# Five of the second pair's eight sets of block sums, made on GpSimd beside the qkv products

## The chip, the cores and the metric

The kernel runs on one core of one Trainium2 chip. The metric is device time in microseconds (us) of one execution. The core's engines are TensorE (PE in the profile: matrix products, with the weight loads listed apart as PEld), VectorE (DVE), ScalarE (ACT), GpSimd (POOL) and SyncE (SP). An engine works through its own instructions strictly in the order in which they stand in its program. A transfer (DMA) is issued by an engine as one of its instructions and then moves on its own; SP does hardly anything but issue transfers.

## The reference

All arrays are fp32: S = 2048 rows, D = 512 columns, Fh = 896.

```python
x  = A_x
xn = layernorm(x)
# s: attention, 32 heads of 16, each row looks at itself and 7 rows before it, 2 apart
q, k, v = split(xn @ wqkv)
logits = einsum("bhsd,bhswd->bhsw", q, k[window]) * scale     # masked before row 0
o  = einsum("bhsw,bhswd->bhsd", softmax(logits), v[window])
s  = o @ wo
# g: gated MLP
z  = gelu_tanh(xn @ w_in)
z1 = z[..., :Fh]
z2 = layernorm(z[..., Fh:])
g  = einsum("ts,bsf->btf", w_sp, z2) + b_sp                    # 2048 x 2048 times 2048 x 896
g  = silu((z1 * g) @ w_out)
out = x + s * g
```

## The kernel before

**Precision.** PE multiplies in a rounded fp32 format. Each operand is therefore split in two (`split`, line 190): ACT copies the high part (line 191), DVE subtracts it to get the low part (line 192), and a product is three matmuls (high by high, high by low, low by high).

**Stages, as PE sees them.** First an opening with the statistics of the rows and the transposes of x, and the products for q, k and v (`qkv`), whose results go to HBM as `qkv_d`. Then the first projection (z1, lines 661 to 682), which stores z1. Then the second projection (z2, lines 692 to 764), whose results are normalised and added up to the combinations that the spatial product needs. Then the spatial product (`g`, `block_product`, matmuls on line 786), then the product with w_out (`b`, line 1009 to 1020), and last `o @ wo` with the final sum (`s`, lines 1046 to 1070).

**The spatial product.** It is done in a scheme of seven block products instead of eight, m1 to m7, for two pairs a = 0, 1 of column blocks of w_sp, in the order m1a m1b m2a m2b m6a m6b m7a m7b m4a m4b m5a m5b m3a m3b. Some of the block products take plain blocks of w_sp (tiles `wsp_...`), the others take sums of blocks (tiles `ws_...`). The sums are made beforehand and kept in HBM as `sums_d`. One set of sums (pair a, index i of eight) loads four blocks of 128x512, makes four DVE additions of 128x512 and stores four results.

**Where the sums are made.** `block_sums(0, i)` for the first pair stands in the loop of the first projection: one set after each f, and the last after the first f; the tiles `sa_...`, `sb_...` are from a wide pool of eight tiles. `block_sums(1, i, False)` for the second pair stands in the loop of the second projection (line 751), one set for each i. Its tiles, `sr_...`, come from the pool `raws`, which has only four buffers ("raw"). `fetch` (line 166) takes one of these buffers and issues the load on SP (line 168). The same four buffers serve the plain blocks and sums of the spatial product (`wsp_...r`, `ws_...r`), the blocks of w_out and wo, and the attention's results on their way to the last stage (`ol`). A set of raw sums takes all four, until its stores have read them.

**The attention.** It runs on DVE, with the first fold of each step on POOL, from q, k, v that are read back from `qkv_d`. There are 32 steps. The large instructions of a step, 128x2048 each, are the product of keys and queries (`pr`, line 523), its reduction (`lg`, line 530) and the product of weights and values (`pv`, line 567); smaller ones are on lines 545 to 561 and 577 to 590. A step's result goes to HBM as `o_d` (issued by SP, line 593). The attention's work has low priority: a scheduler that sorts the program when it is built puts it where it finds DVE free, and the order is fixed then. Its results are needed only by `load_o` (line 766), the operands of the last stage. The last stage takes the row groups in the order 1, 3, 0, 2, and group 3 needs the very last steps of the attention.

**Memory.** The tiles of the opening come from a pool `tmp`: row tiles of x (`t2`, tag "t2", four buffers of 128x512) and others. This memory is released on line 473, and the wide pool and the attention's pool are laid in it. A tile in released memory waits for what used the memory before.

Of the kernel before, what the change touches and what calls it, by code (L numbers as in the profile page):

```python
# [14 lines left out]
ALU = mybir.AluOpType  # L15
AX = mybir.AxisListType

P = 128
S, D, F = 2048, 512, 1792
# [3 lines left out]
NT = S // P  # L23
KB = D // P
FB = FH // P
NG = 3
CT = 512
# [30 lines left out]
def kernel(  # L58
# [16 lines left out]
    def pin(ins):  # L75
        return tc.keep_in_program_order(ins) if pins[0] else ins
# [67 lines left out]
        return t.rearrange("p (k q) -> p k q", k=n)  # L144

    def t2(name, dt=F32, tag="t2", bufs=4):
        return tmp.tile([P, D], dt, tag=tag, name=name, bufs=bufs)

    def t35(name, dt=F32, wide=False):
        return tmp.tile([P, 2 * GC], dt, tag="t35", name=name, bufs=3)[:, : 2 * GC if wide else FH]  # L150
# [42 lines left out]
        return first_  # L193

    def load_x(j):
        xt = t2(f"x_{j}")
        pin(nc.sync.dma_start(xt, xr[j]))
        return xt

# [59 lines left out]
    def rows_ready(j0, j1):  # L259
        v = mvx[:, j0:j1, 1]  # L260
        pin(nc.vector.tensor_scalar(v, v, EPS, None, op0=ALU.add))
        pin(nc.gpsimd.tensor_tensor(v, v, nhalf.to_broadcast([P, j1 - j0]), op=ALU.pow))

    def rows_in(j0, j1):
        mr = ep.tile([P, 4, 2, P], F32, tag="mr", name=f"mr_{j0}", bufs=2)[:, : j1 - j0]
# [23 lines left out]
    def opening(wg):  # L289
        def high(k):  # L290
            hi, lo = weight_pair(f"wqkv_0_{k}")
            pin(nc.scalar.activation(hi, raw[k], AF.Copy))
            wg[k] = hi, lo

        def low(k, eng):
            pin(eng.tensor_tensor(wg[k][1], raw[k], wg[k][0].bitcast(F32), op=ALU.subtract))

        left = [12, 12]

        def times(j, *kab):  # L300
            for k, a, b in kab:
                pin(nc.tensor.matmul(
                    first[j], xn_at(j)[a][:, k], wg[k][b],
                    start=left[j] == 12, stop=left[j] == 1,
                ))
                left[j] -= 1

        x = [load_x(0)]
        raw = [fetch(wqkv[:, 0, 0, :], GC, "wqkv_0_0")]
        x.append(load_x(1))  # L310
        raw += [fetch(wqkv[:, 0, k, :], GC, f"wqkv_0_{k}") for k in (1, 2)]
        raw.append(t35("wqkv_0_3r")[:, :GC])
        pin(nc.sync.dma_start(raw[3], wqkv[:, 0, 3, :]))
        x.append(load_x(2))
        stats_x(0, x[0])
        high(0)
        normal_x(0, x[0])
        low(0, nc.vector)
        p = turned_x(0, x[0])
        stats_x(1, x[1])  # L320
        low_x(0, p)
        high(1)
        normal_x(1, x[1])
        rstd_x(0)
        low(1, nc.vector)
        high(2)
        low(2, nc.gpsimd)
        keep_warm(2)
        first.append(mm("qkv_0_0"))
        times(0, (0, 0, 0), (0, 0, 1))  # L330
        p = turned_x(1, x[1])
        high(3)
        stats_x(2, x[2])
        low(3, nc.gpsimd)
        times(0, (0, 1, 0), (1, 0, 0), (1, 1, 0), (1, 0, 1), (2, 0, 0), (2, 1, 0))
        low_x(1, p)
        normal_x(2, x[2])
        rstd_x(1)
        first.append(mm("qkv_0_1"))
        times(1, *[(k, 0, 0) for k in range(KB - 1)], (0, 0, 1), (1, 0, 1))  # L340
        times(0, (3, 0, 0), (3, 1, 0), (2, 0, 1))
        p = turned_x(2, x[2])
        times(1, (3, 0, 0), *[(k, 1, 0) for k in range(KB)], (2, 0, 1))
        times(0, (3, 0, 1))
        times(1, (3, 0, 1))
        x += [load_x(j) for j in range(3, OPEN)]
        for j in range(OPEN, OPEN + 4):
            fetch_rows(j)
        raw1 = [fetch(wqkv[:, 1, k, :], GC, f"wqkv_1_{k}") for k in range(3)]
        raw1.append(t2("wqkv_1_3r", tag="tz", bufs=2))  # L350
        pin(nc.sync.dma_start(raw1[3], wqkv[:, 1, 3, :]))
        for j in range(3, OPEN):
            xt = x[j]
            stats_x(j, xt)
            low_x(j - 1, p)
            normal_x(j, xt)
            if j - 1 < JC:
                rstd_x(j - 1)
            first.append(mm(f"qkv_0_{j - 1}"))
            left.append(12)  # L360
            times(j - 1, *[(k, 0, i) for i in range(2) for k in range(KB)])
            p = turned_x(j, xt)
            times(j - 1, *[(k, 1, 0) for k in range(KB)])
            row_stats(OPEN + j - 3)
        low_x(OPEN - 1, p)
        for j in range(10, 13):
            fetch_rows(j)
        for j in range(6, 10):
            fetch_cols(j)
        rows_ready(6, 9)  # L370
        rows_out(6, 9)
        return raw1

    def product(g, j, wg):
        xh, xl = xn_at(j)
        pq = mm(f"qkv_{g}_{j}")
        for k in range(KB):
            wh, wl = wg[k]
            nc.tensor.matmul(pq, xh[:, k], wh, start=k == 0, stop=False)  # L379
            nc.tensor.matmul(pq, xh[:, k], wl, start=False, stop=False)  # L380
            nc.tensor.matmul(pq, xl[:, k], wh, start=False, stop=k == KB - 1)  # L381
        return pq

    zpad = tmp.tile([PAD, CS], F32, tag="zpad", name="zpad", bufs=1)
    nc.vector.memset(zpad, 0.0)
# [40 lines left out]
    pair(1, 0)  # L426
    for j in range(13, NT):
        row_stats(j)
    rows_ready(13, NT)
    column_tile(8)  # L430
    low_x(7, cols[7])
    fetch_cols(12)
# [5 lines left out]
    column_tile(10)  # L438
    low_x(9, cols[9])
    pair(1, 4)  # L440
    for j in range(11, NT):
        if j + 2 < NT:
            fetch_cols(j + 2)
        column_tile(j)
        low_x(j - 1, cols[j - 1])
        if j % 2:
            pair(0, j - 5)
# [184 lines left out]

    attention()

    def pair_tiles(a, i):
        top, low = t4(f"sa_{a}_{i}"), t4(f"sb_{a}_{i}")
        nc.sync.dma_start(top, w_sp[2 * a : 2 * a + 2, i].rearrange("c p t -> p c t"))
        nc.sync.dma_start(low, w_sp[2 * a : 2 * a + 2, HT + i].rearrange("c p t -> p c t"))
        return top, low, [top[:, 0], top[:, 1], low[:, 0], low[:, 1]]

    def raw_tiles(a, i):
        return [
            fetch(w_sp[2 * a + c, r + i], CT, f"sr_{a}_{i}_{c}_{r}") for r in (0, HT) for c in range(2)
        ]

    def block_sums(a, i, whole_pairs=True):
        if whole_pairs:
            top, low, ts = pair_tiles(a, i)
        else:
            ts = raw_tiles(a, i)  # L650
        t0, t1, l0, l1 = ts
        for out_, p_, q_ in ((l1, t1, l1), (t1, t0, t1), (t0, t0, l1), (l0, t0, l0)):
            nc.vector.tensor_tensor(out_, p_, q_, op=ALU.add)
        if whole_pairs:
            nc.scalar.dma_start(sums_d[a, 0, i], top)
            nc.scalar.dma_start(sums_d[a, 1, i], low)
        else:
            for n, t in enumerate(ts):
                nc.scalar.dma_start(sums_d[a, n // 2, i, :, n % 2], t)

    for f in range(FB):
        wh, wl = prep(w_in1[:, f, :], KB * P, f"w1_{f}")
        for c in range(NC):
            pz = mm(f"z1_{f}_{c}")
            for k in range(KB):
                cc = slice(k * P, (k + 1) * P)
                xh, xl = [planes[:, FB - KB + k, c * JC : (c + 1) * JC, a] for a in range(2)]
                nc.tensor.matmul(pz, wh[:, cc], xh, start=k == 0, stop=False)  # L668
                nc.tensor.matmul(pz, wh[:, cc], xl, start=False, stop=False)  # L669
                nc.tensor.matmul(pz, wl[:, cc], xh, start=False, stop=k == KB - 1)  # L670
            if c % 2 == 0:
                zp = t4(f"z1t_{f}_{c}")
            zt = zp[:, c % 2]
            if c == 0:
                nc.vector.tensor_tensor(zt, pz, rb, op=ALU.mult)
                pz = zt
            nc.scalar.activation(zt, pz, AF.Gelu_apprx_tanh)
            if c % 2:
                nc.scalar.dma_start(z1_d[f, c - 1 : c + 1].rearrange("c p t -> p c t"), zp)
        block_sums(0, f)  # L680
        if f == 0:
            block_sums(0, FB)

    HALF = (slice(0, 512), slice(512, FH))
    WID = (512, FH - 512)
# [61 lines left out]
    biases = [[b_a[:, 0], b_a[:, 1]]]  # L747
    raw_z = {}
    for i in range(HT + 2):
        if i < HT:  # L750
            block_sums(1, i, False)
            raw_z[i] = [t4(f"zt_{j}").rearrange("p i t -> p (i t)")[:, :FH] for j in (i, HT + i)]
            for h in range(2):
                for j, zt in zip((i, HT + i), raw_z[i]):
                    z2_half(j, h, zt)
                if i == HT - 1 and h == 0:
                    spatial[0, 1] = spatial_block(0, 1)
        if 0 < i <= HT:
            for j, zt in zip((i - 1, HT + i - 1), raw_z[i - 1]):
                z2_stats(j, zt)  # L760
        if i > 1:
            for j, zt, n in zip((i - 2, HT + i - 2), raw_z[i - 2], (ODD + 1, FB)):
                z2_normal(j, zt, n)
            combine(i - 2, raw_z[i - 2])
# [350 lines left out]
```

## Time and profile before

| | us |
|---|---|
| median of 3 runs | 784.45 |
| lowest, highest | 783.91, 784.7 |
| the profiled execution | 783.25 |
| its span | 781.5 |
| DVE busy | 616.8 |
| PE busy | 692.1 |
| POOL busy | 116.3 |

The profile is of one execution. The span is from its first to its last instruction in the trace; its own time is 1.75 us longer. A row of a group of instructions has the line of the program, the engine, the operation, the output and input tiles with the shapes, the number of instructions, then the busy time, the mean of one in nanoseconds, and the idle time of the engine just before them with the instruction that ended it. Digits in the slices are tenths of the slice.

### The profile page before, as it was taken

The numbers are of one execution on the slowest core, as the hardware profiler recorded it, in microseconds if no ns is written. First come the engines' busy times: TensorE is split into PE (matmuls) and PEld (weight loads), VectorE is DVE, ScalarE is ACT, GpSimd is POOL, SyncE is SP. The second block draws the span as 40 slices with busy tenths as digits, with TensorE's granted clock in tenths as the row PEclk, the third lists the DMA queues.
The fourth block names the chain that finished last, engine by engine and source line by source line (L and its number), as shares of the span: only waits on it lengthen the run. The fifth ranks groups of instructions, "written<-read, shape, count | busy, mean of one in ns | idle before, by whom it ended". The sixth has DMA issues, their size and how long they took to land.

```text
span 781.5 us, 9331 instructions
## 1 busy us (share of the span) xinstructions
PE 692.1 (89%) x3084; PEld 574.8 (74%) x3084; DVE 616.8 (79%) x902; ACT 285.0 (36%) x458; POOL 116.3 (15%) x110
## 2 busy tenths in 40 slices
PE   8999999999999994000299999999999999999998
PEld 7888888888888992000288888888888888888886
DVE  6753699999899899989889999989998777110264
ACT  4433332442345558300134343434333444221530
POOL 3100012211215545211112111111100000000000
PEclk9999999999999997555599999999999999999999
DMA  8676876999998266677658997684757765343594
GB/s 296 207 219 199 257 212 183 283 355 371 359 347 297 75 235 179 208 222 236 209 191 287 315 333 260 209 282 158 257 163 226 238 214 177 108 136 147 184 317 185
DMA packets 112512, 182.38 MB, mean 233 GB/s; under 512 B 10576, under 2 KB 50768, under 8 KB 112464
## 3 DMA queue, kind: packets, MB, share of 16 engines
q1 hardware_dynamic: 69408, 130.79, 51.7%
q10 hardware_dynamic: 43056, 50.99, 18.5%
q8 instruction: 24, 0.39, 0.2%
q14 instruction: 24, 0.20, 0.1%
HBM read 122.42 MB, written 59.32 MB: 233 GB/s over the span
## 4 chain that ended last, share of the span: by engine, by line
PE 67%; DVE 13%; DMA 11%; issue 5%; POOL 2%; ACT 1%; SPq 1%; DVEq 0%; ACTq 0%
PE g L786 21%; PE qkv L379 5%; PE qkv L380 5%; PE qkv L381 5%; PE b L1009 3%; PE z L669 3%; PE z L668 3%; PE b L1010 3%; PE b L1011 3%; PE z L670 3%; DVE pr L523 2%; PE s L1011 2%; PE s L1009 2%; PE s L1010 2%; DVE pv L567 2%
## 5 line engine op out<-in xcount | busy, mean ns | idle before, releaser
L577 POOL TENSOR_TENSOR pv<-pv 128x1024 f32<-128x1024 f32 x29 | 69.5, 2395 | 375.0 <-DVE pv L567 306.1
L523 DVE TENSOR_TENSOR pr<-k,q 128x2048 f32<-128x2048 f32 x32 | 73.2, 2286 | 6.4 <-DMA q<-qkv_d 4.4
L786 PE MATMUL g<-wsp_1h,BIG 128*128 128x512 f32 x16 | 7.6, 513 | 79.4 <-ACT wsp_1h L191 79.4
L567 DVE TENSOR_TENSOR pv<-v,lg 128x2048 f32<-128x2048 f32 x32 | 73.1, 2285 | 0.5
L530 DVE TENSOR_REDUCE lg<-pr 128x128 f32<-128x2048 f32 x32 | 72.9, 2277 | 0.0
L786 PEld LDWEIGHTS g<-wsp_1h,BIG 128*128 128x128 f32 x16 | 4.0, 258 | 80.7 <-ACT wsp_1h L191 79.9
L396 ACT ACTIVATE stage<-qkv 128x512 f32<-128x512 f32 x36 | 21.4, 594 | 47.9 <-PE qkv L381 47.9
L192 DVE TENSOR_TENSOR o_1l<-ol,o_1h 128x512 fp32r<-128x512 f32 x3 | 2.1, 688 | 32.9 <-ACT o_1h L191 32.9
L1020 ACT ACTIVATE bt<-b 128x512 f32<-128x512 f32 x16 | 9.5, 596 | 50.1 <-PE b L1011 50.1
L718 ACT ACTIVATE zt<-zt,nmz,mvz 128x896 f32<-128x896 f32 x16 | 18.2, 1135 | 22.6 <-POOL nmz L714 22.5
L553 ACT ACTIVATE lg<-lg 128x256 f32<-128x256 f32 x16 | 6.6, 413 | 53.3 <-DVE tt L590 26.5
L699 PE MATMUL z<-w_0h,BIG 128*128 128x512 f32 x64 | 25.0, 391 | 0.0
L698 PE MATMUL z<-w_0l,BIG 128*128 128x512 f32 x64 | 25.0, 391 | 0.0
L697 PE MATMUL z<-w_0h,BIG 128*128 128x512 f32 x64 | 24.9, 389 | 0.0
L1064 DVE TENSOR_TENSOR sg<-s,sg 128x512 f32<-128x512 f32 (+1 forms) x17 | 11.2, 658 | 16.9 <-PE s L1011 16.9
L275 DVE TENSOR_TENSOR xT<-xT,mr 128x512 f32<-128x512 f32 x20 | 13.8, 688 | 11.4 <-DMA mr<-mv_d 6.5
L191 ACT ACTIVATE BIG<-zl 128x512 fp32r<-128x512 f32 x20 | 12.5, 627 | 26.3 <-DVE zl L851 26.3
L582 DVE TENSOR_TENSOR pv<-pv 128x512 f32<-128x512 f32 x32 | 21.8, 680 | 0.0
L699 PE MATMUL z<-w_1h,BIG 128*128 128x384 f32 x64 | 21.5, 336 | 0.0
L697 PE MATMUL z<-w_1h,BIG 128*128 128x384 f32 x64 | 21.5, 335 | 0.0
L698 PE MATMUL z<-w_1l,BIG 128*128 128x384 f32 x64 | 21.4, 335 | 0.0
L192 DVE TENSOR_TENSOR BIG<-zt,BIG 128x512 fp32r<-128x512 f32 (+2 forms) x24 | 18.5, 770 | 3.1 <-ACT BIG L191 3.1
(464 smaller groups left out, 2270.5 us busy)
## 6 DMA issues: line engine op xcount, KB each, us to landing
qkv_d<-stage ACTq DMA_DIRECT2D x24, 512.0 KB
k<-qkv_d SPq DMA_DIRECT2D x16, 704.0 KB
v<-qkv_d SPq DMA_DIRECT2D x16, 704.0 KB
z_d<-z1t ACTq DMA_DIRECT2D x14, 512.0 KB
zl<-z_d SPq DMA_DIRECT2D x12, 512.0 KB
tr<-t_d SPq DMA_DIRECT2D x12, 384.0 KB
x<-in_x SPq DMA_DIRECT2D x16, 256.0 KB
q<-qkv_d SPq DMA_DIRECT2D x16, 256.0 KB
```

The source lines that it names most:

```text
L379: nc.tensor.matmul(pq, xh[:, k], wh, start=k == 0, stop=False)
L380: nc.tensor.matmul(pq, xh[:, k], wl, start=False, stop=False)
L381: nc.tensor.matmul(pq, xl[:, k], wh, start=False, stop=k == KB - 1)
L523: line(nc.vector.tensor_tensor(pr, taps(ks[u], j0), qb.unsqueeze(1).to_broadcast([P, W, NJ * CS]), op=ALU.mult))
L530: line(nc.vector.tensor_reduce(lgs[u][:, :, j0 * HS : (j0 + NJ) * HS], pr.rearrange("p w (i d) -> p w i d", d=DH), axis=AX.X, op=ALU.add,))
L567: line(nc.vector.tensor_tensor(pv.rearrange("p w (i d) -> p w i d", d=DH), taps(vs[u], j0).rearrange("p w (i d) -> p w i d", d=DH), lgs[u] ...
L577: eng.tensor_tensor(pv[:, 0:4], pv[:, 0:4], pv[:, 4:8], op=ALU.add)
L697: nc.tensor.matmul(pz, xh[:, k], wh, start=k == 0, stop=False)
L698: nc.tensor.matmul(pz, xh[:, k], wl, start=False, stop=False)
L699: nc.tensor.matmul(pz, xl[:, k], wh, start=False, stop=k == KB - 1)
L786: nc.tensor.matmul(pg, z[a], w[b], start=start and i == 0, stop=stop and i == 2, skip_group_check=seeded)
L1009: nc.tensor.matmul(pp[:, cols], hi, wh, start=k == 0, stop=False)
```

## The change

The sets i = 0 to 4 of the second pair are taken out of the second projection. They are issued behind `pair(1, 4)`, in the opening's qkv part, and everything of them is GpSimd's: the two loads of 512 KB, the four additions, and the two stores of 512 KB of each set. Their tiles are `t2` tiles, which are doubled to 128x1024 for it; the tag "tz" goes from two buffers to one. The loads are ordered on GpSimd behind the last statistics of the rows (`rows_known`), without a wait of their own.

The sets 5, 6 and 7 stay as raw sums in the second projection, at i = 1, 3 and 5. The sets of the first pair are now one ahead of the first projection's loop and one behind each f.

```diff
     def t2(name, dt=F32, tag="t2", bufs=4):
-        return tmp.tile([P, D], dt, tag=tag, name=name, bufs=bufs)
+        return tmp.tile([P, 2 * D], dt, tag=tag, name=name, bufs=bufs)
...
-        raw1.append(t2("wqkv_1_3r", tag="tz", bufs=2))
+        raw1.append(t2("wqkv_1_3r", tag="tz", bufs=1)[:, :D])
...
+    def added(ts, eng):
+        t0, t1, l0, l1 = ts
+        for out_, p_, q_ in ((l1, t1, l1), (t1, t0, t1), (t0, t0, l1), (l0, t0, l0)):
+            eng.tensor_tensor(out_, p_, q_, op=ALU.add)
+
+    def block_sums(a, i, tile_=None, eng=nc.vector, loads=nc.sync, stores=nc.scalar):
+        top, low = [(tile_ or t4)(f"s{n}_{a}_{i}") for n in "ab"]
+        for t, r in ((top, 0), (low, HT)):
+            ins = loads.dma_start(t, w_sp[2 * a : 2 * a + 2, r + i].rearrange("c p t -> p c t"))
+            if tile_:
+                tc.add_manual_dep(ins.ins, rows_known.ins.name, NOSYNC, reason="rows first")
+        added([top[:, 0], top[:, 1], low[:, 0], low[:, 1]], eng)
+        for r, t in enumerate((top, low)):
+            stores.dma_start(sums_d[a, r, i], t)
+
+    def raw_sums(a, i):
+        ts = [
+            fetch(w_sp[2 * a + c, r + i], CT, f"sr_{a}_{i}_{c}_{r}") for r in (0, HT) for c in range(2)
+        ]
+        added(ts, nc.vector)
+        for n, t in enumerate(ts):
+            nc.scalar.dma_start(sums_d[a, n // 2, i, :, n % 2], t)
+
+    def early_tile(name):
+        return t2(name).rearrange("p (i t) -> p i t", i=2)
+
+    def early_sums(a, i):
+        block_sums(a, i, early_tile, nc.gpsimd, nc.gpsimd, nc.gpsimd)
+
+    z1_sums = [(0, i) for i in range(HT)]
...
-    rows_ready(13, NT)
+    rows_known = rows_ready(13, NT)
...
     pair(1, 4)
+    for i in range(HT - 3):
+        early_sums(1, i)
...
+    for a, i in z1_sums[:1]:
+        block_sums(a, i)
...
-        block_sums(0, f)
-        if f == 0:
-            block_sums(0, FB)
+        block_sums(*z1_sums[f + 1])
...
     for i in range(HT + 2):
+        if i in (1, 3, 5):
+            raw_sums(1, HT - 3 + i // 2)
         if i < HT:
-            block_sums(1, i, False)
```

The scheduler sorts the changed program anew, and three places show it. A row has the line, the operation and the tiles with the shape.

The first place is on DVE, at the end of the qkv products and the start of the first projection. `wqkv_...l` are the low parts of the last weights of the qkv products, `w_...l` those of the first projection, `z1t` is the first projection's first result, and `pr` the first instruction of a step of the attention. Before:

```order
L229 TENSOR_TENSOR BIG<-xT_588,BIG 128x4x128
L192 TENSOR_TENSOR wqkv_0l<-wqkv_0r,wqkv_0h 128x512
L523 TENSOR_TENSOR pr_0_1160<-k_0_1155,q_0_1156 128x2048
L192 TENSOR_TENSOR wqkv_1l<-wqkv_1r,wqkv_1h 128x512
L192 TENSOR_TENSOR wqkv_2l<-wqkv_2r,wqkv_2h 128x512
L192 TENSOR_TENSOR wqkv_3l<-wqkv_3r,wqkv_3h 128x512
```

And with the change:

```order
L192 TENSOR_TENSOR w_6l<-w_6r,w_6h 128x512
L192 TENSOR_TENSOR w_0_0l<-w_0_0r,w_0_0h 128x512
L685 TENSOR_TENSOR z1t_0_2002<-z_0_0_1989,rb 128x512
L387 TENSOR_TENSOR sb_0_1974<-sa_0_1973,sb_0_1974 128x512
L387 TENSOR_TENSOR sa_0_1973<-sa_0_1973 128x512
L387 TENSOR_TENSOR sa_0_1973<-sa_0_1973,sb_0_1974 128x512
L387 TENSOR_TENSOR sb_0_1974<-sa_0_1973,sb_0_1974 128x512
L556 TENSOR_TENSOR pr_0_1210<-k_0_1205,q_0_1206 128x2048
L192 TENSOR_TENSOR w_1_0l<-w_1_0r,w_1_0h 128x512
```

The attention began behind the first of the last qkv weights; it now begins behind the first result of the first projection and the first set of sums. Before, 8 `pr`, 7 `lg` and 4 `pv` stood ahead of the first `z1t`, and now none.

The second place is on SP, at the end of the raw sums, where the first block of the spatial product (`wsp_1r`) is fetched. Before:

```order
L168 DMA sr_7_0_0r<-in_w_sp 128x512
L593 DMA o_d<-tt_4_1565 32x2x128 x3
L168 DMA sr_7_1_0r<-in_w_sp 128x512
L593 DMA o_d<-tt_4_1565 32x2x128
L168 DMA sr_7_0_8r<-in_w_sp 128x512
L168 DMA sr_7_1_8r<-in_w_sp 128x512
L168 DMA wsp_1r<-in_w_sp 128x512
```

And with the change:

```order
L168 DMA sr_7_0_0r<-in_w_sp 128x512
L168 DMA sr_7_1_0r<-in_w_sp 128x512
L168 DMA sr_7_0_8r<-in_w_sp 128x512
L168 DMA sr_7_1_8r<-in_w_sp 128x512
L626 DMA o_d<-tt_0_1358 32x2x128 x4
L545 DMA v_1_1379<-qkv_d 128x1408
L168 DMA wsp_1r<-in_w_sp 128x512
```

The fetch stood behind the loads of all eight raw sets (32 loads, from `sr_0` to `sr_7`) and now stands behind three (12 loads, `sr_5` to `sr_7`).

The third place is on DVE, behind the splits of w_out's last block and of wo. `o_...l` and `BIG<-ol` are the low parts of the attention's results for the last stage, `sg` its first sums. Before:

```order
L192 TENSOR_TENSOR BIG<-wo_2r,BIG 128x512
L192 TENSOR_TENSOR BIG<-wo_3r,BIG 128x512
L192 TENSOR_TENSOR BIG<-ol_0_5962,BIG 128x512
L192 TENSOR_TENSOR BIG<-ol_1_5967,BIG 128x512
L192 TENSOR_TENSOR BIG<-ol_2_5972,BIG 128x512
L192 TENSOR_TENSOR BIG<-ol_3_5977,BIG 128x512
```

And with the change, some hundred instructions further down than `wo_3r`:

```order
L600 TENSOR_TENSOR pv_0_1951<-v_1_1945,lg_1883 128x2048
L610 TENSOR_TENSOR pv_0_1951<-pv_0_1951 128x1024
L192 TENSOR_TENSOR o_1l<-ol_1_6159,o_1h 128x512
L192 TENSOR_TENSOR BIG<-ol_3_5947,BIG 128x512
L615 TENSOR_TENSOR pv_0_1951<-pv_0_1951 128x512
L192 TENSOR_TENSOR o_2l<-ol_2_6166,o_2h 128x512
L616 TENSOR_TENSOR pv_0_1951<-pv_0_1951 128x4x2x32
L623 STREAM_TRANSPOSE tt_0_1956<-pv_0_1951 128x256
L600 TENSOR_TENSOR pv_4_1962<-v_1_1945,lg_1883 128x2048
L1073 TENSOR_TENSOR sg_5928<-s_0_5989,sg_5928 128x512
```

Before, no instruction of the attention stood behind `wo_3r`. Now 7 `pr`, 8 `lg` and 11 `pv` do, and the last stage's `sg` follow the last `pv` directly.

More of the change, by code (lines that the diff above doesn't have):

```diff
@@ L195, in load_x @@
     def load_x(j):
-        xt = t2(f"x_{j}")
+        xt = t2(f"x_{j}")[:, :D]
         pin(nc.sync.dma_start(xt, xr[j]))
@@ L261, in rows_ready @@
         pin(nc.vector.tensor_scalar(v, v, EPS, None, op0=ALU.add))
-        pin(nc.gpsimd.tensor_tensor(v, v, nhalf.to_broadcast([P, j1 - j0]), op=ALU.pow))
+        return pin(nc.gpsimd.tensor_tensor(v, v, nhalf.to_broadcast([P, j1 - j0]), op=ALU.pow))
     def rows_in(j0, j1):
@@ L633 @@
     attention()
[L635 to L659, printed above, removed]
+    for a, i in z1_sums[:1]:
+        block_sums(a, i)
     for f in range(FB):
```

## The prediction

> **What bounds the kernel now.** I read the page first, for where PE stands still.
>
> ```profile
> span 781.5 us, 9331 instructions
> PE   8999999999999994000299999999999999999998
> DVE  6753699999899899989889999989998777110264
> PEclk9999999999999997555599999999999999999999
> L786 PE MATMUL g<-wsp_1h,BIG 128*128 128x512 f32 x16 | 7.6, 513 | 79.4 <-ACT wsp_1h L191 79.4
> ```
>
> PE is full but for one hole of 79.4 us ahead of the spatial product (slices 16 to 20), which ends when the first block, `wsp_1`, is there. DVE is full from slice 6 to past the middle of the spatial product, and nearly empty in slices 35 to 38. Next, the waits of SP's queue and the chain of waits through the hole (start, length, what):
>
> ```profile
> SPq L168 <- DMA sums_d<-sr_0r: 50.8, 12, 24.7
> 354.05 3.72 DMA sums_d<-sr_8r
> 357.83 2.56 DMA sr_8r<-in_w_sp
> 361.03 2.28 DVE pr L523
> 365.49 5.92 DMA sums_d<-sr_0r
> 372.26 3.19 DMA sr_8r<-in_w_sp
> 380.97 3.70 DMA sums_d<-sr_0r
> 385.59 5.15 DMA wsp_4r<-in_w_sp
> ```
>
> One raw set after another goes round the four buffers: load, four additions between the attention's instructions, store, buffer free, next load. The fetch of `wsp_1` stands behind the last of them on SP. So two things set the hole: this ring, and the work that DVE has in front. Which one ends last after the change is read from DVE's own stages (us, then busy time and instructions of PE, PEld, DVE, ACT, POOL, PE's clock, DMA share, GB/s):
>
> ```profile
> 80.20:147.00 66.80, 66.80 (x296) 55.36 (x295) 61.40 (x71) 20.46 (x35) 9.62 (x4) 1.00 0.74 224
> 147.00:401.60 254.60, 171.62 (x770) 144.46 (x770) 237.45 (x351) 93.75 (x143) 72.00 (x79) 0.83 0.75 258
> 401.60:657.80 256.20, 255.94 (x1129) 211.68 (x1128) 233.36 (x331) 105.62 (x179) 24.48 (x11) 1.00 0.73 241
> 657.80:734.00 76.20, 76.20 (x337) 63.09 (x337) 13.66 (x22) 20.14 (x33) 0.00 (x0) 1.00 0.33 116
> 734.00:781.50 47.50, 43.83 (x205) 36.62 (x203) 26.09 (x35) 12.91 (x17) 0.00 (x0) 0.98 0.77 266
> ```
>
> The stages are cut at rows of DVE's timeline (start, length):
>
> ```profile
> 136.53 2.29 DVE L567 TENSOR_TENSOR pv<-v,lg 128x2048 f32<-128x2048 f32 x1
> 138.74 2.28 DVE L530 TENSOR_REDUCE lg<-pr 128x128 f32<-128x2048 f32 x1
> 147.04 0.68 DVE L675 TENSOR_TENSOR z1t<-z,rb 128x512 f32<-128x512 f32 x1
> 401.61 0.95 DVE L192 TENSOR_TENSOR wsp_7l<-wsp_7r,wsp_7h 128x512 fp32r<-128x512 f32 x1
> 658.93 0.69 DVE L192 TENSOR_TENSOR wout_6l<-wout_6r,wout_6h 128x512 fp32r<-128x512 f32 x1
> ```
>
> From the first result of the first projection (147.04) to `wsp_7` of the first block product (401.61) DVE is busy for 237 of 255 us. PE's 172 us there would fit into far less. DVE is the bound of that stage. From 401.61 on PE is the bound, with DVE close behind it, and from 657.8 DVE has next to nothing.
>
> **The change part by part.** First, what DVE loses: 20 additions of the raw sums. Prices of DVE's instructions, from groups:
>
> ```profile
> L523 DVE TENSOR_TENSOR pr<-k,q 128x2048 f32<-128x2048 f32 x32 | 73.2, 2286 | 6.4 <-DMA q<-qkv_d 4.4
> L567 DVE TENSOR_TENSOR pv<-v,lg 128x2048 f32<-128x2048 f32 x32 | 73.1, 2285 | 0.5
> L653 DVE TENSOR_TENSOR sr_8r<-sr_0r,sr_8r 128x512 f32<-128x512 f32 x16 | 10.8, 673 | 6.3 <-DMA sr_8r<-in_w_sp 3.8 <-issue 2.6
> L192 DVE TENSOR_TENSOR BIG<-zl,BIG 128x512 fp32r<-128x512 f32 x20 | 13.5, 680 | 0.7 <-ACT BIG L191 0.7
> ```
>
> Neighbours overlap: the rows at 136.53 and 138.74 lie 2.21 apart though the first lasts 2.29. I take 0.06 off each instruction: 0.62 us for an addition, 2.22 for a large one of the attention. The 20 additions are 12.4 us. That alone is small against 79.4.
>
> The larger effect is order. Attention that stood ahead of the first projection (8 `pr`, 7 `lg`, 4 `pv` and small ones, 53 us by those prices, in the row from 80.20 to 147.00) now stands behind `z1t`. The reason is memory: the released tiles are now also those of the early sums, so the attention's tiles and the first `sa`, `sb` wait for the early stores. And behind it the order gives the attention less room ahead of the first block product: 10 `pr`, 10 `lg`, 7 `pv` instead of 14, 15, 15. I count the new order in three pieces.
>
> Piece 1, `z1t` to the last operand of the first block product. Before, the instructions there sum to 242.4 us by the prices and took 254.6, a density of 0.95. Now 17 large ones less (37.7), 20 additions less (12.4), 43 small ones of the attention less (18.7), 6 of the combinations and 4 splits that moved behind (5.5), and 13 memsets (0.4): 74.7 us less, so 167.7. At 0.95 that is 176. The first `sb` behind `z1t` waits for 2 MB of loads that are issued only when the early stores are done and the last qkv result is stored; I take 8 us, between 3.19 for one load in the row above and three of 5.15 one behind another (15). Piece 1 ends at 147 + 8 + 176 = 331, where before it was 401.6. The raw ring has 3 sets instead of 8 and so ends well ahead of it.
>
> Piece 2, from there to `wout_6l`: before 236.8 us of work in 257.3, PE being the bound. Now 9 large ones more (20.0), and 5 us of splits, combinations and small ones: 261.9. In the full stretch of the spatial product DVE reached 0.97:
>
> ```profile
> 380.00:400.00 20.00, 14.90 (x53) 11.66 (x54) 17.93 (x21) 6.76 (x11) 2.76 (x2) 0.74 0.81 270
> 400.00:420.00 20.00, 20.00 (x90) 16.55 (x89) 19.56 (x28) 7.85 (x14) 4.41 (x2) 1.00 0.68 213
> ```
>
> 261.9 / 0.97 = 270, to 601. PE needs 256.2, and 3.1 for the low clock after what is left of its hole (53 matmuls at 281 ns in the first row, 222 in the second), so PE ends its last block product at about 592 and then waits for DVE. DVE has become the bound here too, by some 10 us.
>
> Piece 3, the attention's rest, which before had ended ahead of w_out: 8 `pr`, 8 `lg`, 10 `pv` (57.7), small ones and memsets (24.6), 20 splits (12.6), folds and others (3.5), up to the last split that the last stage's first rows need: 98.6 us. Its density is lower, since splits of `ol` stand among these instructions, and each waits for a round trip through HBM:
>
> ```profile
> 340.65 4.95 DMA o_d<-tt
> 730.78 0.69 DVE L192 TENSOR_TENSOR o_1l<-ol,o_1h 128x512 fp32r<-128x512 f32 x1 [32.89 <-ACT o_1h L191]
> ```
>
> Store 4.95, load 3.19, issue and ACT's split some 2.4: 10.5 us. Mostly some 6 us of other work lie between, so three trips leave some 13 bare: I take 11, or 0.90, so 110 us, to 711. Meanwhile PE makes the product with w_out, 16 rows, some 73 us in the row to 734.00, done by about 675; it then waits some 36 us. This is the hole in its new place.
>
> Then the tail, whose end is as before:
>
> ```profile
> 777.87 0.42 DVE L1064 TENSOR_TENSOR sg<-s,sg 128x256 f32<-128x256 f32 x1 [0.55 <-PE s L1011]
> ```
>
> 39 matmuls at 0.222 (8.7, from 90 in 20 us) and the low clock again (3.1), two `sg` (1.3), the last step's fold and transposes (4.9), issue and round trip (10.5), the 135 of the stage's 192 matmuls that are left (30.0 and 3.1), the last sums and store (3.6, from this row to the end of the span): 65. The span ends at 776. The profiled execution's time is 783.25, 1.75 above its span, and the median 1.2 above that: **779 us**. So 66 us gained at the spatial product are given back almost whole ahead of the last stage.
>
> What lies beside the qkv products: the early sums. Their additions and start:
>
> ```profile
> 39.70 1.22 POOL L262 TENSOR_TENSOR mvx<-mvx,nhalf 128x3 f32<-128x3 f32 x1 [7.18 <-DVE mvx L261]
> L296 POOL TENSOR_TENSOR wqkv_3l<-wqkv_3r,wqkv_3h 128x512 fp32r<-128x512 f32 x1 | 1.3, 1292 | 0.0
> L577 POOL TENSOR_TENSOR pv<-pv 128x1024 f32<-128x1024 f32 x29 | 69.5, 2395 | 375.0 <-DVE pv L567 306.1
> ```
>
> They can begin at 41, and must be done by about 147. 20 additions at 1.29 are 26 us. GpSimd's own transfers are not in the trace; from below they are hidden behind the additions of the other buffers (done by 70), from above each of the 20 takes the longest row above, 5.92, with none beside another: 41 + 26 + 118 = 185. I take one load, the additions and one store in turn for each set, 2 x 5.92 + 5.2 = 17, five times: done at 126. PE shows no wait in the qkv part, the DMA share there is 0.74, and the attention's loads go out of it, so the 10 MB more are hidden. Were they not, PE would lose what they are late.
>
> **The rivals.** *The early sums are late.* Everything behind `z1t` hangs on their stores, and DVE has no slack behind it: each us past 147 is a us of the end, and the change loses from 5.4 us on. At the upper bound, 38 us late, it is 817; GpSimd's additions held by DVE's would do it too: 20 times one 2.22 instruction more is 44, done at 170, 23 late, 802. Against it stands the POOL fold, 2395 ns each in 29, beside a DVE that is 95% busy. The Trainium skill, "SBUF — State Buffer", section "Who interferes with whom", speaks for it: DVE's additions of two SBUF operands and GpSimd's reads exclude each other for whole instructions, and GpSimd's transfers can starve for descriptors. By it the time would be near the 802; the even length of the folds does not agree, and of the descriptors no run here shows anything.
>
> *The tail is worse.* If the round trips are bare in piece 3 (six of them at 10.5, less what little stands between), the density is 0.78, 126 us, and the end 795. For it: the `ol` splits stand in DVE's own order, so DVE itself waits, and all `ol` go through the four buffers. It turns slower at a density of 0.855.
>
> *DVE runs through.* With no waits in pieces 1 to 3 (168, 262 and 99), the last operand is there at 684, and the time 752; with a density of 0.97 in all three, 147 + 4 + 173 + 270 + 102 = 696 and 764. For it: 0.97 in the spatial product before. Against: 0.95 in piece 1 before, with its loads on time.
>
> *The change doesn't do what it says*, the hole staying because SP's fetch of `wsp_1` still stands behind `sr_7`: with three sets the ring at its longest turn (24.7 in the row of waits) needs 74 us, well under piece 1's 176. I give this next to nothing.
>
> **How the numbers follow.** The forecast, 768 to 792 (the densities by 0.02 to 0.05 either way, 15 us, a little less as they hardly fall together): 0.52. DVE runs through, under 768: 0.19. Early sums late, 792 to 817: 0.16. The tail worse, 785 to 805: 0.13. Within 0.2% of 784.45 (782.9 to 786.0; what a measurement of this kernel can tell from no change) lies 0.09, all of the forecast's upper part. Faster: 0.35 of the forecast and 0.19, so 0.54. Slower: 0.08, 0.16 and 0.13, so 0.37. The range for 8 in 10, with 0.08 left out below and 0.12 above, is 762 to 800.
>
> **What would show it.** PE's hole ahead of `wsp_1` shrinks from 79 to some 10 us and the last block product ends near 592; if it ends near 640, piece 1 is wrong. POOL's last early store lands by 130, and the first `sb` addition is at about 156; later than 165 means that the sums are late. PE stands still for some 36 us between w_out's product and the last stage, and DVE is nearly full from 150 to 700; if that second hole is under 15 us, the time is under 768. The prediction is wrong at its root if PE waits in the qkv products, or if the spatial product itself has new holes of more than 10 us.

## The result, and the profile after

The change makes the kernel faster: 751.43 us against 784.18 in the same runs, a ratio of 0.9588 (0.9571 to 0.9604). The prediction was 779, with a range of 762 to 800: the direction was right, the size was not.

The page of the changed kernel, to be held against the one of before:

```profile
span 749.5 us, 9288 instructions
PE   8989999999999999799999999999999999990474
DVE  6768310159998999989999999999999999979845
PEclk9989999999999999899999999999999999996698
```

The hole in slices 16 to 20 has shrunk to a dent, and a new one stands in slices 37 and 38. DVE is nearly empty in slices 6 to 8, where the attention had begun before, and full from 10 to 37, where before it had little to do from slice 35 on. The waits of PE (what waited, for what: us in total, times, longest) give the size of both holes, and a wait that was not there before:

```profile
PE s L1018 <- ACT BIG L191: 27.8, 1, 27.8
PE g L795 <- DVE wsp_1l L192: 3.4, 1, 3.4
PE qkv L381 <- DVE BIG L229: 3.2, 2, 2.9
```

The first is the new hole, between w_out's product and the last stage. The second is what is left of the 79.4 us. The third is in the qkv products. The prediction's four pieces, cut at the same instructions (columns as in the stages of before):

```profile
154.25:328.73 174.48, 170.33 (x781) 145.02 (x780) 162.70 (x249) 89.64 (x137) 50.89 (x71) 0.98 0.80 280
328.73:589.69 260.96, 260.96 (x1153) 216.09 (x1152) 255.82 (x362) 110.17 (x183) 33.98 (x15) 1.00 0.77 255
589.69:702.72 113.03, 85.19 (x377) 70.23 (x376) 101.39 (x127) 27.01 (x44) 19.14 (x8) 0.90 0.48 153
702.72:749.50 46.78, 32.01 (x132) 25.42 (x132) 28.81 (x40) 10.59 (x11) 0.00 (x0) 0.86 0.70 261
```

DVE is 93, 98 and 90% busy in the first three; PE works through all of piece 2 without a gap (260.96 of 260.96 us). The product with w_out begins at 582.1 instead of 657.8, so 75.7 us were gained up to there, and 43.7 of them lost again by the end of the span (749.5 against 781.5).

The start of piece 1 in DVE's timeline shows what stands there:

```profile
154.25 0.69 DVE L685 TENSOR_TENSOR z1t<-z,rb 128x512 f32<-128x512 f32 x1 [2.63 <-DMA w_0r<-in_w_in]
159.24 0.69 DVE L387 TENSOR_TENSOR sb<-sa,sb 128x512 f32<-128x512 f32 x1 [4.30 <-DMA sb<-in_w_sp]
163.07 2.29 DVE L556 TENSOR_TENSOR pr<-k,q 128x2048 f32<-128x2048 f32 x1 [0.96 <-DMA q<-qkv_d]
```

`z1t` comes 7.2 us later than before, the loads behind it and in front of the first `pr` cost 5.3 us, and the attention begins at 163 instead of 80. GpSimd's last early store was issued at 104, and SP issued the first load of `k` at 154.9, so it was not that store which the attention waited for:

```profile
104.08 0.56 POOL L397 DMA_DIRECT2D sums_d<-sb  x1
```

### The profile page after: what moved, and what is told of

Same layout as the page of the kernel before. It is cut to its first block, busy times and chain, and to the rows that moved or that the text cites. A ratio compares the mean times of both kernels' runs of the same rounds, so it can differ in the third digit from the quotient of the medians.

```text
span 749.5 us, 9288 instructions
## 1 busy us (share of the span) xinstructions
PE 697.5 (93%) x3084; PEld 578.8 (77%) x3084; DVE 614.3 (82%) x882; ACT 288.8 (39%) x460; POOL 154.4 (21%) x150
## 4 chain that ended last, share of the span: by engine, by line
PE 73%; DVE 13%; DMA 8%; issue 2%; ACT 2%; SPq 1%; POOL 0%; DVEq 0%; ACTq 0%
PE g L795 36%; PE qkv L381 4%; PE qkv L380 4%; PE qkv L379 4%; PE z L679 3%; PE z L678 3%; PE z L680 3%; PE z L707 3%; PE z L706 3%; PE z L705 3%; DMA sg<-b_d 3%; DMA ol<-o_d 2%; DVE pr L556 2%; PE b L1019 2%; PE b L1018 2%
## 5 line engine op out<-in xcount | busy, mean ns | idle before, releaser
L1018 PE MATMUL s<-BIG 128*128 128x512 f32 x16 | 7.3, 459 | 27.8 <-ACT BIG L191 27.8
L275 DVE TENSOR_TENSOR xT<-xT,mr 128x512 f32<-128x512 f32 x20 | 18.0, 899 | 11.8 <-DMA mr<-mv_d 9.3
L1018 PEld LDWEIGHTS s<-BIG 128*128 128x128 f32 x16 | 3.5, 220 | 29.0 <-ACT BIG L191 28.3
L381 PE MATMUL qkv<-wqkv_0h,BIG 128*128 128x512 f32 x43 | 17.5, 407 | 3.2 <-DVE BIG L229 3.2
L795 PE MATMUL g<-ws_0h,BIG 128*128 128x512 f32 x52 | 20.2, 389 | 0.0
L795 PE MATMUL g<-ws_1h,BIG 128*128 128x512 f32 x52 | 20.2, 389 | 0.0
L795 PE MATMUL g<-ws_2h,BIG 128*128 128x512 f32 x52 | 20.2, 389 | 0.0
```

What stands on the lines that cost most here:

```text
L795: nc.tensor.matmul(pg, z[a], w[b], start=start and i == 0, stop=stop and i == 2, skip_group_check=seeded)
L1018: nc.tensor.matmul(pp[:, cols], hi, wh, start=k == 0, stop=False)
```

## The experiments

Two theories on the hole ahead of the spatial product: that it is the amount of DVE's work, or the ring of the raw sets. And two on what the change gives back: the early sums themselves, or the doubled tiles that they came with. The kernels ran on three chips, each beside the kernel before, which took 782.95 to 784.04 us there; the ratios are against that.

**Three sets, nothing early.** In the kernel before:

```diff
-            block_sums(1, i, False)
+            if i > 4:
+                block_sums(1, i, False)
...
-        return lambda s: prep(sums_d[a, half_, s, :, i], ...
+        return lambda s: prep(sums_d[a * (s > 4), half_, s, :, i], ...
```

> The kernel before with the sets 0 to 4 of the second pair left out (the spatial product reads the first pair's sums in their place, so its reads stay); nothing early, memory as before. DVE theory (the hole ahead of the spatial product is DVE's work, and each us taken off is a us gained): 20 additions are 12.4 us, so about 770. Ring theory (the hole is the eight rounds of the four buffers, with SP's fetch behind them): three rounds need under 75 us, the hole goes almost whole, 705 to 725, and with the attention begun at 80 there is no second hole ahead of the last stage.

Measured: 704.80 us, ratio 0.8996 (0.8980 to 0.9011), at the ring theory's bottom end. PE's slices and the attention's `pr` (first and last start behind the durations in ns):

```profile
PE   9999999999999999899999999999989999999997
L523 DVE TENSOR_TENSOR pr<-k,q x32: 2266/2278/2476, 80.4 to 602.9; 128x2048 f32<-128x2048 f32 x32
```

No hole at either place, and the attention begins at 80. So 79 us are to be had from leaving out five sets; the change gets 33.

**The additions alone taken out**, loads and stores kept:

```diff
         for out_, p_, q_ in ((l1, t1, l1), (t1, t0, t1), (t0, t0, l1), (l0, t0, l0)):
-            nc.vector.tensor_tensor(out_, p_, q_, op=ALU.add)
+            if whole_pairs or i > 4:
+                nc.vector.tensor_tensor(out_, p_, q_, op=ALU.add)
```

> The kernel before, the five sets keep their loads and stores through the four buffers, but their 20 additions on DVE are left out. DVE theory: 12 us less, 768 to 774. Ring theory: the ring turns nearly as slowly, since only 4 x 0.62 us of some 20 us a round go, 778 to 784.

Measured: 748.59 us, 0.9554 (0.9540 to 0.9568). Both theories miss. The hole fell from 79.4 to 45.2 us, 34 us for 12.4 us of additions. SP's wait for a buffer of the ring, 50.8 us in total and 24.7 at the longest before, is now:

```profile
SPq L168 <- DMA sums_d<-sr_0r: 35.3, 12, 8.0
```

The longest round is gone. The likely reason, read from the chain of waits of before and not tried by itself, is that a set holds its buffers from its first addition to its last, with the attention's instructions of 2.2 us between them. The order also has 8 of the attention's large instructions less ahead of `wsp_1`'s low part (52 instead of 60).

**The additions alone left in**, on a resident tile:

```diff
-            block_sums(1, i, False)
+            if i > 4:
+                block_sums(1, i, False)
+            else:
+                for _ in range(4):
+                    nc.vector.tensor_tensor(b_a[:, 0], b_a[:, 0], b_a[:, 0], op=ALU.max)
...
-        return lambda s: prep(sums_d[a, half_, s, :, i], ...
+        return lambda s: prep(sums_d[a * (s > 4), half_, s, :, i], ...
```

> The kernel before without the five sets' loads and stores, but with 20 additions of the same size on DVE in their place (on a resident tile). DVE theory: 780 to 785, nothing gained. Ring theory: 715 to 740.

Measured: 742.66 us, 0.9481 (0.9464 to 0.9499), between the two. But the experiment was flawed, as its rows for that tile and PE's waits show:

```profile
L755 DVE TENSOR_TENSOR b_a<-b_a x20: 626/676/928, 243.3 to 341.0; 128x512 f32<-128x512 f32 x20
L808 ACT ACTIVATE g<-b_a x5: 579/582/586, 342.3 to 416.4; 128x512 f32<-128x512 f32 x5
```

```profile
PE g L790 <- ACT g L808: 34.2, 1, 34.2
```

The tile holds the spatial product's bias, ACT seeds the product with it, and so PE waited for the last of these 20 instructions. It says nothing of the ring. The same was tried again without this:

**Three sets, and 20 more instructions in the attention**, where nothing but the attention waits for them (the edit of the run with three sets, and):

```diff
+            if 2 * u + j0 // NJ < 20:
+                line(nc.vector.tensor_tensor(pr[:, 0:2], pr[:, 0:2], pr[:, 0:2], op=ALU.max))
             line(nc.vector.tensor_tensor(pr[:, 0:2], pr[:, 0:2], pr[:, 2:4], op=ALU.add))
```

> The kernel before with five sets left out (704.8 us) and the same 20 instructions in the attention, so the additions' DVE time without their loads and stores, and on no tile that another engine waits for. If PE has become the bound there: 704 to 709. If the additions' DVE time itself brings back a hole, as the run on the resident tile (742.7) could be read: 735 to 745.

Measured: 708.56 us, 0.9046 (0.9030 to 0.9062). 3.8 us more for 12.4 us of work, and no hole. So the time that 20 additions take on DVE does not make the hole. It is not without effect: `wsp_1`'s low part comes at 309.5 us instead of 301.9.

What leaves with five sets is more than their additions. These are the stretches from the first `z1t` to `wsp_1`'s low part, in the kernel before and with three sets (columns as in the stages of before):

```profile
147.04:386.18 239.14, 156.17 (x713) 132.38 (x712) 224.07 (x335) 88.12 (x135) 69.61 (x78) 0.82 0.75 258
146.84:301.88 155.04, 151.52 (x704) 129.58 (x703) 146.33 (x227) 72.10 (x110) 47.78 (x56) 1.00 0.82 288
```

DVE is 94% busy in both, and has 77.7 us less to do in the second, close to the hole's 79.4. The additions are 12.4 of them; most of the rest is attention, of whose large instructions 41 stand in the first stretch and 24 in the second. The likely reading, which no run tries by itself, joins the two theories: the sets on the ring keep the fetch of `wsp_1` back, and the order, fixed beforehand, fills DVE's time up to there with attention. How much of the hole the ring would leave without the attention between its additions stays open.

**The changed kernel with the early sums left out**, same order on DVE:

```diff
     pair(1, 4)
-    for i in range(HT - 3):
-        early_sums(1, i)
...
-        return lambda s: prep(sums_d[a, half_, s, :, i], ...
+        return lambda s: prep(sums_d[a * (s > 4), half_, s, :, i], ...
```

> The changed kernel with the early sums left out (the first pair's sums are read in their place); DVE's order is the same row for row. If the early sums cost the 7 us that the first projection starts later (154.2 instead of 147.0): 743 to 746. If they are hidden, and the 7 us come from something else: 750 to 752. If the last stage sets the end whatever the start is: 751.

Measured: 744.03 us, 0.9495 (0.9478 to 0.9511): 7.4 us are the early sums' price. The kernel does the same work as the one with three sets and is 39 us slower. Its `pr` rows:

```profile
L554 DVE TENSOR_TENSOR pr<-k,q x32: 2271/2281/2472, 156.2 to 665.9; 128x2048 f32<-128x2048 f32 x32
```

The attention is as late as in the changed kernel, with no early sum there. What is left of the change is the doubled tiles and the place of the first pair's sums; the run with small tiles, below, keeps that place.

**The early sums without GpSimd's additions:**

```diff
-        added([top[:, 0], top[:, 1], low[:, 0], low[:, 1]], eng)
+        if not tile_:
+            added([top[:, 0], top[:, 1], low[:, 0], low[:, 1]], eng)
```

> The changed kernel with the early sums' loads and stores on GpSimd's queue, but without the 20 GpSimd additions (what is stored is plain blocks). If the 7.4 us of the early sums come from GpSimd's additions holding DVE's (DVE's 128x512 ones take 1.7 to 1.9 us beside them instead of 0.69): 744 to 747, and no DVE row of the opening over 1 us. If they come from the transfers (the load of the row statistics arrives 3.3 us later): 749 to 752.

Measured: 745.81 us, 0.9535 (0.9507 to 0.9562). The medians would give 5.6 us to GpSimd's additions and 1.8 to the transfers, but they are from different chips. The start of `z1t` tells the same with less room: 154.2 in the changed kernel, and here and without early sums:

```profile
149.50 0.69 DVE L686 TENSOR_TENSOR z1t<-z,rb 128x512 f32<-128x512 f32 x1 [2.62 <-DMA w_0r<-in_w_in]
147.36 0.69 DVE L683 TENSOR_TENSOR z1t<-z,rb 128x512 f32<-128x512 f32 x1 [2.61 <-DMA w_0r<-in_w_in]
```

So some 5 us are the additions and 2 the transfers. DVE's group of the column work (`xT`) in the changed kernel, and here:

```profile
L275 DVE TENSOR_TENSOR xT<-xT,mr 128x512 f32<-128x512 f32 x20 | 18.0, 899 | 11.8 <-DMA mr<-mv_d 9.3 <-DMA xT<-in_x_t 2.1
```

```profile
L275 DVE TENSOR_TENSOR xT<-xT,mr 128x512 f32<-128x512 f32 x20 | 13.8, 689 | 22.5 <-DMA xT<-in_x_t 13.0 <-DMA mr<-mv_d 9.1
```

**The doubled tiles alone**, in the kernel before:

```diff
-        return tmp.tile([P, D], dt, tag=tag, name=name, bufs=bufs)
+        return tmp.tile([P, 2 * D], dt, tag=tag, name=name, bufs=bufs)
...
-        xt = t2(f"x_{j}")
+        xt = t2(f"x_{j}")[:, :D]
...
-        raw1.append(t2("wqkv_1_3r", tag="tz", bufs=2))
+        raw1.append(t2("wqkv_1_3r", tag="tz", bufs=1)[:, :D])
```

> The kernel before with nothing but the tiles of x doubled (and one buffer of the other tag instead of two): all eight raw sets stay, no early sums. If the doubled tiles alone push the attention behind the start of the first projection: the first product of keys and queries at 155 to 165 instead of 80. Time: if the total of DVE's work behind that point decides, that of the changed kernel without its early sums (744) and 12.4 us for 20 additions, 754 to 760; if the ring's eight rounds decide, a hole of 70 us or more is left and the time is 780 to 800.

Measured: 775.93 us, 0.9918 (0.9899 to 0.9936), between the two; the hole is the one that the ring's eight rounds were to leave.

```profile
L523 DVE TENSOR_TENSOR pr<-k,q x32: 2270/2280/2294, 152.4 to 666.6; 128x2048 f32<-128x2048 f32 x32
```

```profile
PE g L786 <- ACT wsp_1h L191: 79.4, 1, 79.4
```

The doubled tiles, with the one buffer of "tz" less, push the attention from 80 to 152. How they do it is not shown: in the order, SP's first load of `k` now stands behind the first projection's weights, and is issued at 146.9. The hole is 79.4 us as before; it begins and ends 6 us earlier, and PE's later stages move with it. This does not part the theories. The 19 large instructions of the attention that were moved had stood ahead of `z1t`; between `z1t` and `wsp_1`'s low part stand 42, where before it were 41, and DVE has about as much to do there as before (221.6 us, then 224.1):

```profile
147.17:379.97 232.80, 153.00 (x713) 131.19 (x712) 221.63 (x329) 89.35 (x134) 65.25 (x76) 0.84 0.76 266
```

In this kernel the late attention costs nothing, since it runs beside PE's work behind the hole; without the hole there is no such room, and it must come at the end.

**Small tiles for the early sums:** the five sets early on GpSimd as in the change, but in tiles of 128x512, with five buffers instead of four:

```diff
-    def t2(name, dt=F32, tag="t2", bufs=4):
-        return tmp.tile([P, 2 * D], dt, tag=tag, name=name, bufs=bufs)
+    def t2(name, dt=F32, tag="t2", bufs=5):
+        return tmp.tile([P, D], dt, tag=tag, name=name, bufs=bufs)
...
     def early_sums(a, i):
-        block_sums(a, i, early_tile, nc.gpsimd, nc.gpsimd, nc.gpsimd)
+        ts = [t2(f"se_{a}_{i}_{c}_{r}") for r in (0, HT) for c in range(2)]
+        for n, t in enumerate(ts):
+            ins = nc.gpsimd.dma_start(t, w_sp[2 * a + n % 2, n // 2 * HT + i])
+            tc.add_manual_dep(ins.ins, rows_known.ins.name, NOSYNC, reason="rows first")
+        added(ts, nc.gpsimd)
+        for n, t in enumerate(ts):
+            nc.gpsimd.dma_start(sums_d[a, n // 2, i, :, n % 2], t)
```

> The changed kernel with the same five early sets on GpSimd, but in tiles of 128x512 (five buffers), not doubled; so 40 transfers of 256 KB. If the doubled tiles cost 39 us (744.0 against 704.8): the attention begins at about 80 again, no hole ahead of the last stage, 708 to 718. If the attention beside the early sums loses what it gains (GpSimd's folds stand behind the sums, its additions hold DVE's): 720 to 740.

Measured: 715.51 us, 0.9137 (0.9122 to 0.9152): 36 us faster than the change, with all of its work. The attention begins at 91, and there is no second hole; its `pr` and PE's slices:

```profile
L559 DVE TENSOR_TENSOR pr<-k,q x32: 2270/2278/3199, 91.2 to 615.3; 128x2048 f32<-128x2048 f32 x32
PE   8998999999999799998999999999999999999997
```

It is 10.7 us above the kernel with three sets. **Issued later**, behind the last columns, it was to avoid the collision with DVE:

```diff
     pair(1, 4)
-    for i in range(HT - 3):
-        early_sums(1, i)
...
     low_x(NT - 1, cols[NT - 1])
+    for i in range(HT - 3):
+        early_sums(1, i)
     pair(0, 12)
```

> As the one with small tiles, but the early sums issued behind the last columns of the opening instead of behind the tenth. If the collision with DVE's column work at 50 to 67 us costs the most of the 7 us: 3 to 6 us faster than the one with small tiles. If the sums are then late for the first projection, or the order on GpSimd hardly differs: the same or slower.

Measured: 719.23 us, 0.9188 (0.9170 to 0.9206). It is 3.7 us slower, and PE's wait for the first projection's weights grew from 3.8 to 7.9 us.

**Four early sets in small tiles, four raw:**

```diff
-    for i in range(HT - 3):
+    for i in range(4):
...
-        if i in (1, 3, 5):
-            raw_sums(1, HT - 3 + i // 2)
+        if i in (1, 2, 3, 5):
+            raw_sums(1, {1: 4, 2: 5, 3: 6, 5: 7}[i])
```

> The kernel with small tiles, four early sets instead of five, and four raw sets in the second projection (at i = 1, 2, 3 and 5). If the early sums cost their share in the opening (10.7 us for five against none): 2 us less, about 713.5. If a fourth raw set brings back the hole ahead of the spatial product (no hole was left with three): 720 to 730.

Measured: 731.40 us, 0.9340 (0.9324 to 0.9355). The fourth raw set brings the hole back:

```profile
PE g L798 <- ACT wsp_1h L191: 13.7, 1, 13.7
```

From this to the eight sets of before it is (79.4 - 13.7) / 4 = 16 us for each further set, an estimate, as the two kernels differ in more than the ring.

**The changed kernel with 20 more instructions in the attention** (the same lines as with three sets):

> The changed kernel with 20 more DVE instructions of 128x512 that change nothing (a maximum of a part of the attention's product with itself), one in each of the first 20 steps of the attention: 20 x 0.62 = 12.4 us of DVE work. If DVE's work from the first projection to the attention's end sets the time, as the prediction had it: 762 to 765 and the hole ahead of the last stage 12 us longer (about 40). If something else sets it and DVE has slack: 751 to 754.

Measured: 768.15 us, 0.9811 (0.9790 to 0.9831). 16.7 us more, where the kernel with three sets took the same work for 3.8. PE waits for the attention's results ahead of the last stage, so in the changed kernel DVE sets the end:

```profile
PE s L1020 <- ACT BIG L191: 29.6, 1, 29.6
PE s L1020 <- ACT o_0h L191: 7.7, 1, 7.7
```

The wait ahead of the last stage is 37 instead of 28 us, in two parts. That the time grew by more than the 12.4 us of the instructions stays open; the scheduler set the order anew, and `wout_6l` came 5.7 us later, the rest behind it.

**All eight sets early, doubled tiles:**

```diff
-    for i in range(HT - 3):
+    for i in range(8):
...
-        if i in (1, 3, 5):
-            raw_sums(1, HT - 3 + i // 2)
```

> The changed kernel (doubled tiles) with all eight sets early and none in the second projection. DVE has 12 additions less (7.4 us), GpSimd 12 more (by 5.6 us for 20 of them, 3.4 in the opening), and the last early store comes at about 143 instead of 105. If the sums are still in time: 746 to 749. If they are late for the first projection: 752 or more.

Measured: 743.44 us, 0.9490 (0.9476 to 0.9504), 8.0 us less than the change and better than expected. The last store is issued at 137.6 and the first `z1t` comes at 154.0, as in the change: the three further sets cost nothing in the opening, and DVE's 12 additions less are worth somewhat more than their 7.4 us.

## Why the prediction was wrong

**Right: the first hole goes.** "PE's hole ahead of `wsp_1` shrinks from 79 to some 10 us": 3.4. That the raw ring with three sets is no bound any more held too: with three sets and nothing early no hole is left, and with four one of 13.7 us is back. And the prediction had counted the attention that leaves DVE's order there, not the additions alone: 74.7 us less work for DVE ahead of the first block product. With three sets in the ring DVE has 77.7 us less in nearly the same stretch.

**Right: DVE carries the end, and a second hole opens ahead of the last stage.** Foreseen were 36 us, with w_out's product done by 675; it is 27.8, from 674.7 on. That the start fits is luck: w_out's product is done at 658.4, in part because PE did not wait for DVE at the end of the spatial product as foreseen (some 10 us), and PE then does 72 matmuls of the last stage before it stands still. The run with 20 more instructions confirms that DVE's work sets the end here.

**Missed: the opening.** The early sums were costed at nothing beside the qkv products. They cost 7.4 us, and `z1t` came at 154.2, not 147. PE waits 3.2 us for DVE in the qkv products, which the prediction had named as a sign that it is wrong at its root. The prediction took the POOL fold's even 2395 ns as a sign that GpSimd and DVE do not hold each other. It looked at the engine that is hardly held. Here is the collision in the changed kernel, DVE's row and GpSimd's:

```profile
52.27 3.45 DVE L275 TENSOR_TENSOR xT<-xT,mr 128x512 f32<-128x512 f32 x2
```

```profile
53.56 1.61 POOL L387 TENSOR_TENSOR sa<-sa,sb 128x512 f32<-128x512 f32 x1
```

DVE needs 3.45 us for two where it took 1.41, and it feeds PE at this point. The Trainium skill, "SBUF — State Buffer", section "Who interferes with whom", has this rule, that DVE's two-operand instructions and GpSimd's reads exclude each other. The prediction set it aside; the trace agrees that the two hold each other, though not for whole instructions: one of each takes some 1.7 us, less than the 1.98 of both in turn (0.69 and 1.29). What it did to the time was some 5 us and not the 23 of the rival, since mainly the first sets met DVE at work.

**Wrong in its reason: why the attention is late.** The prediction put it on the early stores, for which the released memory waits. The runs show that the doubled tiles do it, with no early sum and no early store (152.4 and 156.2 us for the first `pr`). The effect that was read from the order, the attention behind `z1t`, was right; that it could be had without it was not seen.

**Mis-sized, in small: pieces 1 to 3.** Predicted 184, 270 and 110, measured 174.5, 261.0 and 113.0. In piece 1 the waits behind `z1t` were 5.3 instead of 8, and the rest is that the sum of DVE's work came out some 2 to 3% too long (162.7 and 255.8 busy, against 167.7 and 261.9). With the later start, the last split that the last stage needs stands at 702.7, not 711.

**The step that failed: the tail.** "39 matmuls [...], two `sg`, the last step's fold and transposes, issue and round trip, the 135 of the stage's 192 matmuls that are left": 65 us, measured 46.8. This is 18 of the 26.5 us between the predicted span of 776 and the measured one (the rest: +7.2, -9.5, -9.0, +3.0). Two of its terms were wrong, and 10 of the 18 us lie ahead of the last operand, 8 behind it. DVE's last `sg` and fold were put behind PE's 39 matmuls; they began 5.0 us behind the split, and the last operand was there 18.4 us behind it instead of 29:

```profile
702.72 0.68 DVE L192 TENSOR_TENSOR BIG<-ol,BIG 128x512 fp32r<-128x512 f32 x1
707.67 2.48 DVE L1073 TENSOR_TENSOR sg<-s,sg 128x512 f32<-128x512 f32 x4
721.15 0.69 DVE L192 TENSOR_TENSOR o_3l<-ol,o_3h 128x512 fp32r<-128x512 f32 x1 [6.06 <-ACT o_3h L191]
```

And PE did far more of the stage beforehand than was counted. These are the instructions of the last stage's result `s` alone (PE, PEld, DVE, then PE's clock, DMA share, GB/s), ahead of the new hole, behind it, and from the last operand on:

```profile
658.20:674.72 16.52, 16.48 (x72) 13.32 (x71) 0.00 (x0) 1.00 0.47 145
702.54:720.50 17.96, 16.21 (x60) 12.58 (x60) 2.48 (x4) 0.88 0.45 154
721.10:740.00 18.90, 15.97 (x72) 13.01 (x72) 6.44 (x10) 0.91 0.95 358
```

The stage has 204 matmuls, not 192, since the last row is made in two halves. 72 of them ran ahead of the new hole, 60 while the last result made its trip, and only 72 were left, 24 of these of half the width; the prediction had 135 left. A row takes three matmuls for each of four operands, so three quarters of it can be made before the last operand comes. PE did this for the first two row groups (1 and 3) ahead of the hole, and made all of the third (0) while the last operand of group 3 made its trip.

The time came out where the third rival, that DVE runs through, had put it (752), though not by its way: the last split that the stage's first rows need, the rival's "last operand", stands at 703, nearer to the forecast's 711 than to the rival's 684.

## What to carry to other kernels

A fetch that stands behind a ring of few buffers comes later with each tile set that goes through the ring, by more than the set's own work: here five sets were 12.4 us of additions and 79 us of time. Count the rounds ahead of the fetch that the waiting engine needs, and what other work the order lets in between them. When work is moved into another memory, ask who is laid into that memory later; here tiles twice as large cost 36 us, five times the 7.4 us that the moved work cost beside them. And for a last stage, count how many of its instructions can run before the last operand comes.

## What was not expected of the hardware

Beside GpSimd's additions of two operands, DVE's instructions of 128x512 with two operands took 1.7 to 1.9 us instead of 0.69, while GpSimd's own went from 1.29 to 1.6. DVE pays most of it. Transfers that GpSimd issues itself were not starved beside it: each load took 0.70 to 0.96 us of GpSimd's time, each store 0.55 to 0.58, and all 20 together, without the additions, moved the first projection by some 2 us.
